# Attention in turns of four key blocks instead of pairs of heads, ahead of a feed-forward network

## The chip, the core and the metric

The kernel runs on one core of one Trainium2 chip. The metric is device time in microseconds of one execution. Engines: PE is TensorE (matmuls; PEld is its weight load), DVE is VectorE, ACT is ScalarE, SP is SyncE, which here only issues transfers (DMAs).

## What is computed

```python
# q, k, v: (8 batches, 12 heads, 448 positions, 64)
scores = scale * np.matmul(q, k.transpose(0, 1, 3, 2)) - np.log(S)
attn = 1.0 / (1.0 + np.exp(-scores))
attn_out = np.matmul(attn, v)
x = attn_out.transpose(0, 2, 1, 3).reshape(B * S, H * D)   # 3584 x 768
h = x @ w_in                                               # 768 x 2048
g = np.maximum(0.01 * h, h)
out = g @ w_out                                            # 2048 x 768
```

The sigmoid takes the place of a softmax, so no sum over keys is needed, and key blocks can be taken in any order.

## The kernel before

Two heads of one batch make a **pair**; there are 48 pairs (`Pair`, from line 348). The 448 keys of a head are three **blocks** of 128 (c = 0, 1, 2) and a rest of 64. For one block PE computes the scores of both heads, side by side in two row halves of the array (64x128 tiles, `sc<-qks`), from q and k split into a high and a low part (high by high, high by low, low by high: three products, so six matmuls a block). ACT takes the sigmoid of both heads at once from PSUM into SBUF (`attn`, line 414, `s<-sc`), and PE multiplies it with v into an accumulator of the pair (`attn_v`, line 427, `pv<-s,v`, 128x64 tiles, two heads side by side). The rests of 64 keys of two neighbouring pairs go together, as four **quarters** of the array (64x64 tiles): `last_scores` (line 419, `sc<-qk`, unsplit) and, in `attn_v`, the products of the rests with v (`pv<-s` on 64x64).

PSUM holds three buffers for scores (`s`, two banks each) and two accumulators (`pv`); the buffers go round in the order in which they are asked for. SBUF holds four raw pairs of q and k (`raws`), two split pairs (`spl`) and six sigmoid blocks (`at`).

The split of a pair is a cast (`high`, line 374, `qks<-qk`, on ACT or, where the plan says so, on DVE) and a subtraction on DVE (`low`, line 378, `qks<-qk,qks`). When a pair's accumulator is complete, ACT copies it to SBUF (`keep`, line 442, `x<-pv`). SP issues all loads (`load_qk`, `load_v`).

The order is written by hand. Every engine works through its own queue in program order. The main loop goes over pairs j, four **slots** each: block 2 of pair j, blocks 0 and 1 of pair j+1, products of pair j with v for blocks 0 and 1, and `ending` (line 646: the product for block 2, and for every second pair the quarters). `later(n, ...)` puts a side task n slots on; `go` (line 637) emits the side tasks that are due, then the slot's matmuls, then as much of `prep()` as `PACES` says: `prep` decodes and sums the weights of the feed-forward network on DVE (`wd`, `ws`) for a product scheme with seven products (`ORDER`). `PLAN_ATTN` puts casts, subtractions and sums of the finished attention outputs (`hi`, `lo`) into slots, `EARLY` calls `advance`, which starts loads and splits of the first weights, in the last pairs.

After the attention comes the feed-forward network: first `x @ w_in` (`px_h`, `py_h`, `pz_h`), then the product with `w_out` (`px_o`, ...); PSUM banks are shared out anew. At the very end the last output block is copied from PSUM by ACT (`c_o<-px_o`) and stored by SP.

Of the kernel before, what the change touches and what calls it, by code (L numbers as in the profile page):

```python
# [27 lines left out]
PACES = 2.2, 2  # L28
# [23 lines left out]
def attn_ffn_kernel(ctx: ExitStack, tc: tile.TileContext, qk, v, w_in, w_out, out):  # L52
# [194 lines left out]
    def give(name):  # L247
# [8 lines left out]
        ("raws", 4), ("spl", 2), ("at", 6)))  # L256
# [91 lines left out]
    class Pair:  # L348


        def __init__(self, i):
            self.i, self.part = i, part(i)
            self.a = []
# [40 lines left out]
        def scores(self, h):  # L394
            todo, acts = [], []
            for c in range(2 * h, min(2 * h + 2, NK - 1)):
                ps = psum("s", f"sc_{self.i}_{c}")

                for cols in HALVES if self.i == h == 0 else (slice(0, S),):
                    for m, (kp, qp) in enumerate(((0, 0), (0, 1), (1, 0))):  # L400
                        for j, me in enumerate(heads):
                            todo.append((c, (m > 0 and c + 1, m, cols.start), dict(
                                out=ps[:, j, cols], lhsT=self.parts[me, kp, 1, c * P:c * P + P],
                                rhs=self.parts[me, qp, 0, cols], start=m == 0 and cols.start == 0,
                                stop=m == 2 and cols.stop == S, skip_group_check=True)))
                acts.append((c, ps))
            if self.i == h == 0:
                todo.sort(key=lambda x: x[1])
            for n, (c, ps) in enumerate(acts):
                for x in todo if self.i == h == 0 and n == 0 else [x for x in todo if x[0] == c and (self.i or h)]:  # L410
                    mm(**x[2])
                self.a.append(self.attn(c, ps))
# [14 lines left out]
        def attn_v(self, h):  # L427
            if h == 0:
                self.pv = psum("pv", f"pv_{self.i}")
            for c in range(2 * h, min(2 * h + 2, NK - 1)):  # L430
                for j, me in enumerate(heads):
                    mm(self.pv[me, :S], lhsT=self.v[:, (NK - 1) * j + c, :], rhs=self.a[c][:, j], start=c == 0, stop=False,
                       skip_group_check=True)
            if h == 1 and self.part == 2:
                x = pairs[self.i - 1]
                for j, me in enumerate(heads):
                    for y, rows in ((x, heads[0]), (self, heads[1])):
                        mm(y.pv[me, :S], lhsT=self.v[rows, 2 * NK - 2 + j, :], rhs=x.last[rows, j],
                           start=False, stop=True, skip_group_check=True)
                later(1, x.keep, self.keep, first=True)  # L440
# [10 lines left out]
    class Operands:  # L451
# [60 lines left out]
        "e13.1": "h002", "e15.1": "l002", "e17.1": "h102", "e19.1": "l102", "e20.1": "s302", "e22.1": "s202", "e24.1": "s402",  # L512
        "e26.1": "s102", "e27.1": "h402", "e29.1": "l402", "e30.1": "h502", "e32.1": "l502", "e33.1": "h302", "e35.1": "l302"}
# [18 lines left out]
    EARLY = {(-4, 0): -8, (-4, 2): -6, (-3, 0): -4, (-2, 0): -3, (-1, 0): -2, (-1, 2): -1, (0, 0): 0}  # L532
# [113 lines left out]
    def ending(j):  # L646

        pairs[j].attn_v(1)
        x = 0 if j == 0 else j + 1
        if x % 2 == 0 and x < last:  # L650
            pairs[x].last_scores()

# [3 lines left out]
    slot(lambda: pairs[0].scores(0))  # L656
    for j in range(last + 1):
# [7 lines left out]
        if j + 4 <= last:  # L665
            later(4, pairs[j + 4].load_qk)
# [112 lines left out]
    for k, (p, n, u0) in enumerate(items):  # L779
# [7 lines left out]
        def work():  # L787
# [7 lines left out]
            for m, (acc, begins) in enumerate(accs):  # L795
# [3 lines left out]
                if ending:  # L799
                    store(p, m, quads[m].done(n))  # L800
# [46 lines left out]
```

## Time and profile before

| | us |
|---|---|
| median of 3 runs (lowest to highest) | 1071.53 (1071.09 to 1071.82) |
| the profiled execution | 1071.87 |
| its span in the trace | 1070.1 |
| busy: PE | 1063.6 (99%) |
| busy: PE weight load | 884.0 (83%) |
| busy: DVE | 672.1 (63%) |
| busy: ACT | 581.4 (54%) |

The profile's page comes from one execution of 1071.87 us. The span runs from the first to the last recorded piece of work. Matmuls follow each other in a pipeline, so that the start of one to the start of the next says more than the duration of one. PE's granted clock is full throughout.

### The profile page before, as it was taken

What the parts mean: (1) busy time and instruction counts of PE and PEld (TensorE: products, weight loads), DVE (VectorE), ACT (ScalarE), POOL (GpSimd) and SP (SyncE); (2) the same over time, 40 slices, a digit from 0 to 9 for tenths busy, and PEclk for the clock granted to TensorE, in tenths of its full rate; (3) what the DMA queues carried; (4) which work ended last, traced back from release to release, by engine and by line L of the source; (5) the groups of instructions that cost most, each with busy time, mean ns of one, the idle gap of its engine ahead of it and who ended that gap; (6) DMA issues with size and microseconds to landing.
All of it is one profiled execution on the core that took longest, in us unless ns stands there. A gap on an engine that the chain in (4) does not pass through costs nothing.

```text
span 1070.1 us, 16067 instructions
## 1 busy us (share of the span) xinstructions
PE 1063.6 (99%) x5882; PEld 884.0 (83%) x5882; DVE 672.1 (63%) x1020; ACT 581.4 (54%) x833; POOL 0.3 (0%) x5
## 2 busy tenths in 40 slices
PE   8999999999999999999999999999999999999998
PEld 5454444545999999999999999999999999999997
DVE  5667878676797898878977666655332423333332
ACT  6787878877554655566555555554333233323332
POOL 0000000000000000000000000000000000000000
PEclk9999999999999999999999999999999999999999
DMA  7787688788899789899898887876544545465552
GB/s 246 251 300 273 240 292 291 254 309 310 247 292 309 210 283 321 273 294 342 256 313 270 265 268 241 318 265 212 184 152 127 184 147 163 121 185 151 152 158 87
DMA packets 107791, 255.61 MB, mean 239 GB/s; under 512 B 11968, under 2 KB 55744, under 8 KB 107712
## 3 DMA queue, kind: packets, MB, share of 16 engines
q1 hardware_dynamic: 107280, 254.13, 72.5%
q8 instruction: 46, 0.75, 0.3%
q10 hardware_dynamic: 432, 0.46, 0.1%
q14 instruction: 33, 0.27, 0.1%
HBM read 167.38 MB, written 87.16 MB: 238 GB/s over the span
## 4 chain that ended last, share of the span: by engine, by line
PE 99%; DMA 1%; DVE 0%; ACTq 0%; ACT 0%; issue 0%; DVEq 0%
PE px_h L85 22%; PE px_o L85 22%; PE pv L85 13%; PE pz_h L85 11%; PE pz_o L85 11%; PE sc L85 11%; PE py_h L85 5%; PE py_o L85 5%; DMA qk<-in_qk 1%; DVE qks L85 0%; ACTq L85 0%; ACT c_o L85 0%; DVEq L85 0%
## 5 line engine op out<-in xcount | busy, mean ns | idle before, releaser
L85 DVE TENSOR_TENSOR gs<-gg,gs 128x896 fp32r<-128x896 f32 x112 | 122.3, 1092 | 226.8 <-ACT gs L85 226.8
L85 PE MATMUL px_o<-gs,w 128*128 128x448 f32 x1152 | 232.5, 362 | 0.0
L85 PE MATMUL px_h<-hi,w 128*128 128x448 f32 x768 | 231.7, 362 | 0.0
L85 PEld LDWEIGHTS px_o<-gs,w 128*128 128x128 f32 x1152 | 216.0, 187 | 14.4
L85 ACT CAST gs<-gg 128x896 fp32r<-128x896 f32 x112 | 105.3, 941 | 220.7 <-PE px_o L85 114.8
L85 ACT ACTIVATE s<-sc 128x896 f32<-128x896 f32 x168 | 150.2, 935 | 47.1 <-PE sc L85 47.1
L85 PEld LDWEIGHTS px_h<-hi,w 128*128 128x128 f32 x768 | 144.0, 187 | 9.7 <-issue 0.7
L85 PE MATMUL pv<-s,v 128*64 128x448 f32 (+1 forms) x768 | 140.7, 551 | 0.0
L85 PE MATMUL px_h<-lo,w 128*128 128x448 f32 x384 | 138.8, 362 | 0.0
L85 DVE TENSOR_TENSOR w<-wx,w 128x768 fp32r<-128x768 f32 (+1 forms) x160 | 136.0, 852 | 3.3 <-ACT w L85 2.8
L85 ACT CAST w<-wx 128x768 fp32r<-128x768 f32 (+1 forms) x160 | 119.6, 751 | 7.1 <-DMA wx<-t 7.0
L85 PE MATMUL pz_h<-hi,w 128*128 128x448 f32 x384 | 118.3, 362 | 0.0
L85 PE MATMUL pz_o<-gs,w 128*128 128x448 f32 x576 | 116.5, 362 | 0.0
L85 PEld LDWEIGHTS pz_o<-gs,w 128*128 128x128 f32 x576 | 108.0, 187 | 7.2
L85 PEld LDWEIGHTS sc<-qks 64*128 64x128 f32 x876 | 76.5, 185 | 42.7 <-issue 31.7
L85 PEld LDWEIGHTS pv<-s,v 128*64 128x64 f32 (+1 forms) x768 | 42.1, 135 | 76.1 <-issue 67.4
L85 PE MATMUL sc<-qks 64*128 64x448 f32 (+1 forms) x876 | 101.8, 373 | 1.8 <-DVE qks L85 1.7
L85 DVE TENSOR_TENSOR qks<-qk,qks 128x832 fp32r<-128x832 f32 (+3 forms) x51 | 49.5, 973 | 56.7 <-ACT qks L85 56.5
L85 ACT COPY c_h<-px_h 128x448 f32<-128x448 f32 x64 | 34.2, 534 | 91.1 <-PE px_h L85 87.6
L85 PEld LDWEIGHTS px_h<-lo,w 128*128 128x128 f32 x384 | 72.0, 187 | 5.4
L85 PEld LDWEIGHTS pz_h<-hi,w 128*128 128x128 f32 x384 | 72.0, 187 | 4.5
L85 DVE SCALAR_TENSOR_TENSOR wd<-wr,wd 128x384 int32<-128x384 int32 x128 | 71.3, 557 | 3.3
(49 smaller groups left out, 951.7 us busy)
## 6 DMA issues: line engine op xcount, KB each, us to landing
gg<-g SPq DMA_DIRECT2D x112, 448.0 KB, 3.5
wx<-t SPq DMA_DIRECT2D x120, 384.0 KB, 4.4
g<-c_h SPq DMA_DIRECT2D x128, 224.0 KB, 4.5
g<-s SPq DMA_DIRECT2D x96, 224.0 KB, 4.5
qk<-in_qk SPq DMA_DIRECT2D x46, 448.0 KB, 5.3
wr<-in_w_in SPq DMA_DIRECT2D x32, 384.0 KB, 3.7
t<-ws SPq DMA_DIRECT2D x16, 768.0 KB, 6.7
wr<-in_w_out SPq DMA_DIRECT2D x32, 384.0 KB, 4.0
```

Of the source, the lines that this page charges most:

```text
L85: return lambda *args, **kw: tc.keep_in_program_order(issue(*args, **kw))
```

## The change

The loop over pairs becomes a loop over 36 **turns** of four key blocks; blocks are numbered through all pairs (block n is block n % 3 of pair n // 3). Turn r has four slots: scores of blocks 4r+1 and 4r+2; scores of 4r+3 and 4r+4; `middle`; products with v of blocks 4r+2 and 4r+3. `middle` emits, in the turns with r % 3 = 0 or 2, the quarters (products of the rests of two pairs with v, then scores of the rests of the next two pairs), and then the products with v of blocks 4r and 4r+1. So the quarters stand between scores and products with v, and no longer between products with v and scores. Turn 0 has an order of its own: the first pair's blocks, the quarters' scores of pairs 0 and 1, the first pair's products with v, then scores of blocks 3 and 4 and `middle`; of the first pair only block 0 is computed in two halves of the columns.

Splits, loads and copies are put into slots by a table (`calls`), copies of accumulators by `DONE`. There are fewer slots, and `prep` gets 2.955 instead of 2.2 steps a slot, which is the same total. `at` has seven buffers. The last output block is copied in two halves, one by ACT, one by DVE, and stored by SP's queue and by ACT's.

```diff
-PACES = 2.2, 2
+PACES = 2.955, 2
...
-        ("raws", 4), ("spl", 2), ("at", 6)))
+        ("raws", 4), ("spl", 2), ("at", 7)))
...
-            self.a = []
+            self.a, self.pv = [], None
...
-        def scores(self, h):
...
+        def scores(self, c):
+            ps = psum("s", f"sc_{self.i}_{c}")
+            cut = HALVES if self.i == c == 0 else (slice(0, S),)
+            for m, (kp, qp) in enumerate(((0, 0), (0, 1), (1, 0))):
+                for cols in cut:
+                    for j, me in enumerate(heads):
+                        mm(ps[:, j, cols], lhsT=self.parts[me, kp, 1, c * P:c * P + P], rhs=self.parts[me, qp, 0, cols],
+                           start=m == 0 and cols.start == 0, stop=m == 2 and cols.stop == S, skip_group_check=True)
+            self.a.append(self.attn(c, ps))
 
...
-        def attn_v(self, h):
...
+        def sums(self):
+            first = self.pv is None
+            if first:
                 self.pv = psum("pv", f"pv_{self.i}")
-            for c in range(2 * h, min(2 * h + 2, NK - 1)):
-                for j, me in enumerate(heads):
-                    mm(self.pv[me, :S], lhsT=self.v[:, (NK - 1) * j + c, :], rhs=self.a[c][:, j], start=c == 0, stop=False,
+            return self.pv, first
+        def attn_v(self, c):
+            pv, first = self.sums()
+            for j, me in enumerate(heads):
+                mm(pv[me, :S], lhsT=self.v[:, (NK - 1) * j + c, :], rhs=self.a[c][:, j], start=first, stop=False,
+                   skip_group_check=True)
+        def last_v(self):
+            y = pairs[self.i + 1]
+            sums = [x.sums() for x in (self, y)]
+            for j, me in enumerate(heads):
+                for (pv, first), rows in zip(sums, heads):
+                    mm(pv[me, :S], lhsT=y.v[rows, 2 * NK - 2 + j, :], rhs=self.last[rows, j], start=first, stop=True,
                        skip_group_check=True)
-            if h == 1 and self.part == 2:
-                x = pairs[self.i - 1]
-                for j, me in enumerate(heads):
-                    for y, rows in ((x, heads[0]), (self, heads[1])):
-                        mm(y.pv[me, :S], lhsT=self.v[rows, 2 * NK - 2 + j, :], rhs=x.last[rows, j],
-                           start=False, stop=True, skip_group_check=True)
-                later(1, x.keep, self.keep, first=True)
 
...
-        "e13.1": "h002", "e15.1": "l002", "e17.1": "h102", "e19.1": "l102", "e20.1": "s302", "e22.1": "s202", "e24.1": "s402",
-        "e26.1": "s102", "e27.1": "h402", "e29.1": "l402", "e30.1": "h502", "e32.1": "l502", "e33.1": "h302", "e35.1": "l302"}
+        "r10.2": "h002", "r11.2": "l002", "r13.2": "h102", "r14.2": "l102", "r15.2": "s302", "r16.2": "s202", "r18.2": "s402",
+        "r19.2": "s102", "r21.2": "h402", "r22.2": "l402", "r23.2": "h502", "r24.2": "l502", "r25.2": "h302", "r26.2": "l302"}
...
-    EARLY = {(-4, 0): -8, (-4, 2): -6, (-3, 0): -4, (-2, 0): -3, (-1, 0): -2, (-1, 2): -1, (0, 0): 0}
+    EARLY = {(-3, 0): -8, (-3, 2): -6, (-2, 0): -4, (-2, 1): -3, (-2, 2): -2, (-1, 0): -1, (-1, 2): 0}
...
-    def ending(j):
-        pairs[j].attn_v(1)
-        x = 0 if j == 0 else j + 1
-        if x % 2 == 0 and x < last:
-            pairs[x].last_scores()
...
-    slot(lambda: pairs[0].scores(0))
-    for j in range(last + 1):
-        works = [lambda: pairs[j].scores(1)] + [lambda: pairs[j + 1].scores(0)] * (j < last)
-        works += [lambda: pairs[j].attn_v(0), lambda: ending(j)]
-        if j + 2 <= last:
-            later(0, pairs[j + 2].load_v)
-            later(1, lambda j=j: pairs[j + 2].high(vcopy if PLAN_ATTN.get(f"e{j}.1", "").startswith("h") else copy))
-            later(2, pairs[j + 2].low)
-        if j + 4 <= last:
-            later(4, pairs[j + 4].load_qk)
+    TURNS = (last + 1) * 3 // 4
+    def run(blocks, kind):
+        for n in blocks:
+            if n < 3 * (last + 1):
+                getattr(pairs[n // 3], kind)(n % 3)
+    def middle(r, blocks):
+        p, n = divmod(r, 3)
+        if n != 1:
+            me = 4 * p + n
+            pairs[me].last_v()
+            if me + 2 < last:
+                pairs[me + 2].last_scores()
+        run(blocks, "attn_v")
+    DONE = {(0, 3): (0,), (1, 2): (1,), (2, 2): (2,), (2, 3): (3,)}
+    calls = {}
+    def call(r, n, fn):
+        calls.setdefault((r, n), []).append(fn)
+    for i in range(2, last + 1):
+        p, n = divmod(i, 4)
+        r, one, two = ((-1, 0, 0), (-1, 2, 3), (0, 2, 3), (1, 2, 3))[n]
+        r += 3 * p
+        call(r, one, lambda i=i, how=vcopy if PLAN_ATTN.get(f"r{r}.2", "").startswith("h") else copy: pairs[i].high(how))
+        call(r, two, pairs[i].low)
+        if i >= 4:
+            r, at_slot = ((0, 2 * (p == 1)), (0, 1 + 2 * (p == 1)), (1, 0), (2, 0))[n]
+            call(3 * p - 3 + r, at_slot, pairs[i].load_qk)
+        r, at_slot = ((1, 0), (1, 3), (2, 3), (3, 0))[n]
+        call(*((3 * p - 3 + r, at_slot) if i >= 4 else (i - 2, 0)), pairs[i].load_v)
+    slot(lambda: run((0,), "scores"))
+    for r in range(TURNS):
+        works = [lambda: run((4 * r + 1, 4 * r + 2), "scores"), lambda: run((4 * r + 3, 4 * r + 4), "scores")]
+        works += [lambda: middle(r, (4 * r, 4 * r + 1)), lambda: run((4 * r + 2, 4 * r + 3), "attn_v")]
+        if r == 0:
+            works = [works[0], pairs[0].last_scores, lambda: run((0, 1), "attn_v"), lambda: run((2,), "attn_v"),
+                     works[1], lambda: middle(0, (3,))]
+            later(len(works), pairs[0].keep, first=True)
         for n, work in enumerate(works):
-            go([(ops[0], PLAN_ATTN.get(f"e{j}.{n}", ""))], work, PACES[0] * (j > 0))
-            t = EARLY.get((j - last, n))
+            later(0, *calls.get((r, n), ()))
+            go([(ops[0], PLAN_ATTN.get(f"r{r}.{n}", ""))], work, PACES[0] * (r > 0))
+            if r and (r % 3, n) in DONE:
+                later(0, *(pairs[4 * (r // 3) + x].keep for x in DONE[r % 3, n]), first=True)
+            t = EARLY.get((r - TURNS, n))
             if t is not None:
                 advance(t)
 
...
-                if ending:
+                if ending and m < NB - 1:
                     store(p, m, quads[m].done(n))
+                elif ending:
+                    t = op.tile([P, S], F32, tag="o", name="end", bufs=8)
+                    b = 2 * p
+                    for cols, how, queue in zip(HALVES, (copy, vcopy), (dma, dma_act)):
+                        how(out=t[:, cols], in_=acc[:, cols])
+                        queue(out=out[NB + m, :, b * S + cols.start:b * S + cols.stop], in_=t[:, cols])
 
```

In the rows below, a name like `sc_17_0` is the score buffer of pair 17, block 0 (block 3: the rests), `s_` its sigmoid, `qks_` a pair's split q and k, `pv_` its accumulator; the last number of a name only tells buffers apart.

PE's queue before, two pairs in the middle of the attention:

```order
L85 MATMUL sc_16_2_1137<-qks_16_1027 128x448 x6
L85 MATMUL sc_17_0_1150<-qks_17_1079 128x448 x6
L85 MATMUL sc_17_1_1151<-qks_17_1079 128x448 x6
L85 MATMUL pv_16_1169<-s_16_0_1091,v_16_1014 64x448 x2
L85 MATMUL pv_16_1169<-s_16_1_1099,v_16_1014 64x448 x2
L85 MATMUL pv_16_1169<-s_16_2_1144,v_16_1014 64x448 x2
L85 MATMUL sc_17_2_1180<-qks_17_1079 128x448 x6
L85 MATMUL sc_18_0_1197<-qks_18_1148 128x448 x6
L85 MATMUL sc_18_1_1198<-qks_18_1148 128x448 x6
L85 MATMUL pv_17_1218<-s_17_0_1158,v_17_1066 64x448 x2
L85 MATMUL pv_17_1218<-s_17_1_1166,v_17_1066 64x448 x2
L85 MATMUL pv_17_1218<-s_17_2_1187,v_17_1066 64x448 x2
```

PE's queue after, from turn 13 to the scores of turn 14:

```order
L85 MATMUL sc_17_2_1197<-qks_17_1081 128x448 x6
L85 MATMUL sc_18_0_1206<-qks_18_1166 128x448 x6
L85 MATMUL sc_18_1_1218<-qks_18_1166 128x448 x6
L85 MATMUL sc_18_2_1227<-qks_18_1166 128x448 x6
L85 MATMUL pv_17_1169<-s_17_1_1162,v_17_1022 64x448 x2
L85 MATMUL pv_17_1169<-s_17_2_1204,v_17_1022 64x448 x2
L85 MATMUL pv_18_1255<-s_18_0_1213,v_18_1106 64x448 x2
L85 MATMUL pv_18_1255<-s_18_1_1225,v_18_1106 64x448 x2
L85 MATMUL sc_19_0_1269<-qks_19_1240 128x448 x6
L85 MATMUL sc_19_1_1278<-qks_19_1240 128x448 x6
L85 MATMUL sc_19_2_1290<-qks_19_1240 128x448 x6
L85 MATMUL sc_20_0_1299<-qks_20_1264 128x448 x6
```

Before, three blocks of scores alternate with three blocks of products; after, four alternate with four, and block 0 of pair 20 is computed ahead of the products of pair 19.

ACT's queue before, around the splits of pairs 44 and 45:

```order
L85 COPY x_13_2518<-pv_41_2604 128x448
L85 ACTIVATE s_42_2_2640<-sc_42_2_2633 128x896
L85 CAST qks_44_2646<-qk_44_2565 128x832
L85 ACTIVATE s_43_0_2656<-sc_43_0_2648 128x896
L85 ACTIVATE s_43_1_2664<-sc_43_1_2649 128x896
L85 ACTIVATE s_43_2_2692<-sc_43_2_2685 128x896
L85 CAST qks_45_2698<-qk_45_2629 128x832
```

ACT's queue after, turn 31 (four sigmoids) and the beginning of turn 32:

```order
L85 ACTIVATE s_41_2_2593<-sc_41_2_2586 128x896
L85 ACTIVATE s_42_0_2602<-sc_42_0_2595 128x896
L85 ACTIVATE s_42_1_2615<-sc_42_1_2608 128x896
L85 ACTIVATE s_42_2_2624<-sc_42_2_2617 128x896
L85 CAST qks_43_2629<-qk_43_2425 128x832
L85 COPY x_13_2506<-pv_41_2555 128x448
L85 CAST qks_44_2652<-qk_44_2510 128x832
L85 ACTIVATE s_43_0_2664<-sc_43_0_2657 128x896
```

Before, each pair's cast stands between the sigmoids of one pair and the next; after, the cast of pair 43 follows four sigmoids in a row, and the cast of pair 44 follows it with one copy between.

DVE's queue before, from the subtraction of pair 43 to that of pair 44 (`wd` is `prep`'s work):

```order
L85 TENSOR_TENSOR qks_43_2580<-qk_43_2520,qks_43_2580 128x832
L85 TENSOR_SCALAR wd1_2_2562<-wr1_2_1_2449 128x384
L85 TENSOR_SCALAR wd1_2_2562<-wd1_2_2562 128x384 x2
L85 SCALAR_TENSOR_TENSOR wd1_2_2562<-wr1_2_1_2449,wd1_2_2562 128x384 x2
L85 TENSOR_SCALAR wd1_2_2562<-wr1_2_2_2495 128x384
L85 TENSOR_SCALAR wd1_2_2562<-wd1_2_2562 128x384 x2
L85 TENSOR_TENSOR qks_44_2646<-qk_44_2565,qks_44_2646 128x832
```

DVE's queue after, the same two subtractions:

```order
L85 TENSOR_SCALAR wd1_2_2571<-wr1_2_2_2490 128x384
L85 TENSOR_TENSOR qks_43_2629<-qk_43_2425,qks_43_2629 128x832
L85 TENSOR_SCALAR wd1_2_2571<-wd1_2_2571 128x384 x2
L85 SCALAR_TENSOR_TENSOR wd1_2_2571<-wr1_2_2_2490,wd1_2_2571 128x384
L85 TENSOR_TENSOR qks_44_2652<-qk_44_2510,qks_44_2652 128x832
L85 SCALAR_TENSOR_TENSOR wd1_2_2571<-wr1_2_2_2490,wd1_2_2571 128x384
```

Before, five groups of `prep`'s instructions stand between the two subtractions; after, two.

## Rows read from the trace of the kernel before

**Rows 1.** Page, chain that ended last: share of the span by engine.

```profile
PE 99%; DMA 1%; DVE 0%; ACTq 0%; ACT 0%; issue 0%; DVEq 0%
```

**Rows 2.** Busy time by stretch: PE, PEld, DVE, ACT, POOL; clock; DMA share; GB/s.

```profile
50.00:100.00 50.00, 50.00 (x368) 25.22 (x362) 34.44 (x68) 40.19 (x53) 0.00 (x0) 1.00 0.77 267
```

**Rows 3.** PE's timeline: start, length, work, count [idle before]; two pairs.

```profile
92.23 0.93 PE L85 MATMUL sc<-qk 64*64 64x448 f32 x8
...
95.11 2.48 PE L85 MATMUL pv<-s,v 128*64 128x448 f32 x12
97.52 2.09 PE L85 MATMUL sc<-qks 64*128 64x448 f32 x18
99.54 3.39 PE L85 MATMUL pv<-s,v 128*64 128x448 f32 x20
102.74 0.93 PE L85 MATMUL sc<-qk 64*64 64x448 f32 x8
```

**Rows 4.** PE's timeline, end of the attention.

```profile
255.62 0.88 PE L85 MATMUL sc<-qks 64*128 64x448 f32 x6
256.42 3.39 PE L85 MATMUL pv<-s,v 128*64 128x448 f32 x20
259.74 0.47 PE L85 MATMUL px_h<-hi,w 128*128 128x448 f32 x1
```

**Rows 5.** Weight loads' timeline, products with v and quarters.

```profile
99.96 0.14 PEld L85 LDWEIGHTS pv<-s,v 128*64 128x64 f32 x2 [0.23 <-issue]
...
101.09 0.14 PEld L85 LDWEIGHTS pv<-s,v 128*64 128x64 f32 x2 [0.23 <-issue]
101.94 0.21 PEld L85 LDWEIGHTS pv<-s,v 64*64 64x64 f32 x8 [0.70 <-issue]
102.37 0.15 PEld L85 LDWEIGHTS sc<-qk 64*64 64x64 f32 x4 [0.22 <-issue]
```

**Rows 6.** PE's timeline, first scores.

```profile
3.98 2.64 PE L85 MATMUL sc<-qks 64*128 64x224 f32 x30
```

**Rows 7.** Chain of waits at the start: start, length, what.

```profile
1.65 5.38 DMA qk<-in_qk
```

**Rows 8.** The load of q and k issued at 6.9: issue and landing.

```profile
L85 SPq DMA_DIRECT2D qk<-in_qk x1: 328/328/328, 6.9 to 6.9; - x1
...
DMA to landing us min/median/max: 6.4/6.4/6.4
```

**Rows 9.** ACT's timeline beside rows 3.

```profile
95.77 0.91 ACT L85 CAST qks<-qk 128x832 fp32r<-128x832 f32 x1
...
98.49 0.93 ACT L85 ACTIVATE s<-sc 128x896 f32<-128x896 f32 x1 [0.18 <-PE sc L85]
...
100.51 1.73 ACT L85 ACTIVATE s<-sc 128x896 f32<-128x896 f32 x2
```

**Rows 10.** Timeline of all engines, a score run that waits for a sigmoid.

```profile
171.14 2.15 PE L85 MATMUL sc<-qks 64*128 64x448 f32 x18
...
172.41 0.50 PEld L85 LDWEIGHTS sc<-qks 64*128 64x128 f32 x6 [0.16 <-ACT s L85]
```

**Rows 11.** DVE's timeline beside rows 3.

```profile
96.71 1.03 DVE L85 TENSOR_TENSOR qks<-qk,qks 128x832 fp32r<-128x832 f32 x1 [1.24 <-ACT qks L85]
...
99.12 0.76 DVE L85 TENSOR_SCALAR wd<-wd 128x384 f32<-128x384 f32 x2
...
100.37 1.15 DVE L85 SCALAR_TENSOR_TENSOR wd<-wr,wd 128x384 int32<-128x384 int32 x2
```

**Rows 12.** SP's loads of q and k, from 15 to 260 us: issue to landing.

```profile
DMA to landing us min/median/max: 3.9/5.3/9.7
```

**Rows 13.** ACT's timeline, the last copy.

```profile
1066.48 0.53 ACT L85 COPY c_o<-px_o 128x448 f32<-128x448 f32 x1 [0.67 <-PE px_o L85]
```

**Rows 14.** The last two stores: issue to landing.

```profile
DMA to landing us min/median/max: 1.9/1.9/1.9
```

**Rows 15.** Page, DMA issues: count, KB each, median us to landing.

```profile
qk<-in_qk ACTq DMA_DIRECT2D x2, 112.0 KB, 2.8
```

More of the change, by code (lines that the diff above doesn't have):

```diff
@@ L392, in split @@
                         sub(low[:, 0, x], self.raw[:, 0, x], high[:, 0, x])
-        def scores(self, h):
-            todo, acts = [], []
-            for c in range(2 * h, min(2 * h + 2, NK - 1)):
-                ps = psum("s", f"sc_{self.i}_{c}")
-                for cols in HALVES if self.i == h == 0 else (slice(0, S),):
-                    for m, (kp, qp) in enumerate(((0, 0), (0, 1), (1, 0))):
-                        for j, me in enumerate(heads):
[L402 to L412, printed above, removed]
+        def scores(self, c):
[7 more added lines that the diff above has]
+            self.a.append(self.attn(c, ps))
         def attn(self, c, ps):
@@ L425, in last_scores @@
             self.last = self.attn(NK - 1, ps)
-        def attn_v(self, h):
-            if h == 0:
+        def sums(self):
+            first = self.pv is None
+            if first:
                 self.pv = psum("pv", f"pv_{self.i}")
-            for c in range(2 * h, min(2 * h + 2, NK - 1)):
-                for j, me in enumerate(heads):
-                    mm(self.pv[me, :S], lhsT=self.v[:, (NK - 1) * j + c, :], rhs=self.a[c][:, j], start=c == 0, stop=False,
-                       skip_group_check=True)
-            if h == 1 and self.part == 2:
-                x = pairs[self.i - 1]
-                for j, me in enumerate(heads):
-                    for y, rows in ((x, heads[0]), (self, heads[1])):
-                        mm(y.pv[me, :S], lhsT=self.v[rows, 2 * NK - 2 + j, :], rhs=x.last[rows, j],
-                           start=False, stop=True, skip_group_check=True)
-                later(1, x.keep, self.keep, first=True)
+            return self.pv, first
[10 more added lines that the diff above has]
+                    mm(pv[me, :S], lhsT=y.v[rows, 2 * NK - 2 + j, :], rhs=self.last[rows, j], start=first, stop=True,
+                       skip_group_check=True)
         def keep(self):
```

## The prediction

> **What bounds the kernel now.** I read the chain that ended last first: it runs through PE for 99% of the span [rows 1], so a change is worth what it takes from PE's queue, less the waits that it puts there. Then a stretch of the attention: PE is busy all the time, DVE 69% and ACT 80% of it [rows 2]; these two have room on average, and the question is whether they are in time at each place. Then PE's timeline over two pairs [rows 3], which gives the price of each step, and the end of the attention [rows 4]: the feed-forward network starts at 259.74. From there only the last block is changed, so the sum is the new time of that start, and the tail.
>
> **Prices.** From start to start, six score matmuls take 256.42 - 255.62 = .80 [rows 4] and eighteen 99.54 - 97.52 = 2.02 [rows 3]. So a block of scores is .61 and a run of them .20 more. A step of products with v (both heads, half of a block) is (101.09 - 99.96) / 3 = .376 [rows 5]; six steps take 97.52 - 95.11 = 2.41 [rows 3], so a run costs .16 beside its steps, and a block .75. The extra is the change of tiles: from the step at 101.09 to the first one on 64x64 tiles are .85 [rows 5], two steps and .10, and that first one takes .43, .05 more than a step. A change to fp32 tiles is thus .15; the run of scores, with the changes at both its ends, shows .20. The quarters are four steps: two of products and two of scores, and between them there is no change (102.37 - 101.94 and 102.74 - 102.37 [rows 3, 5]). With their changes they add (3.20 - 2.41) + .87 = 1.66, with 102.74 - 99.54 = 3.20 and .87 from the rest.
>
> Two pairs are one period of 102.74 - 92.23 = 10.51 [rows 3], so four pairs take 21.02. By the prices: 12 blocks of scores 7.29, 12 of products 9.02, eight quarter steps 3.01, four runs of each kind 1.44, two changes for quarters .33; together 21.1, which agrees.
>
> **Part 1, longer runs.** After the change four pairs are three turns: three runs of each kind instead of four, which is .36 less in 21.02. A turn without quarters is 4 x .61 + .20 + 4 x .75 + .16 = 5.8 (5.78 unrounded), with quarters 7.45 (+1.67). For this the quarters stand between scores and products with v: scores to 64x64 and 64x64 to 128x64 are two neighbourhoods that no row shows. Bounds: nothing for both, or .20 each; I take .15 and .16, which is the nearest change shown, 128x64 to 64x64 [rows 5].
>
> A sentence of the Trainium skill, page "TensorEngine Tiling (Array Packing)", section "Key Properties", says that changing the tiling mode, not just the tile, drains the engine. By it the two unseen changes cost what the shown ones do and the sum stays; without it rival 2 holds. The trace agrees where it shows changes (.15, .20).
>
> **Part 2, the start.** Scores of pair 0 still end near 3.98 + 2.64 = 6.62 [rows 6]. The quarters of pairs 0 and 1 need the load that lands at 1.65 + 5.38 = 7.03 [rows 7]; with a weight load PE starts at 7.2, ends at 8.07. Products of pair 0 (2.41) to 10.48; blocks 0 and 1 of pair 1 (1.41) to 11.89, products of the rests (.80) to 12.69. The next quarters need the q and k issued at 6.9, landing 6.4 later, at 13.3 [rows 8]; from 13.35 their scores take .87 and the block that follows .91: turn 1 starts at 15.13. Turns 1 to 35: 12 x 5.78 + 23 x 7.45, less 1.36 for the last one (three blocks of scores, no scores of rests), is 239.35. **Without new waits the attention ends at 254.5, 5.25 earlier than now.**
>
> **Part 3, the waits that it adds.** Let T be a turn's start.
> (a) *The score banks.* There are three, so the fourth block of a run takes the first one's. A sigmoid starts .97 after its run (98.49 - 97.52), lasts .93 [rows 3, 9], so the bank is free at T + 1.90 and the weight load can go .05 later. Without a wait that load would be at T + 1.72: the load of the third block of a run begins, in [rows 10], at 172.41 - 171.14 = 1.27, of which .16 is such a wait, so 1.11, and a block is .61 more. It is thus .23 late. In [rows 10] a load that was .16 late made the run only .06 longer (2.15 against 2.09 [rows 3]), so PE has .10 of lead: .13 a run. Bounds: 0 (ACT was earlier free than that) and .22. For 34 runs **4.4** (0 to 7.5).
>
> The same page, section "PSUM Bottleneck", warns that tiling makes TensorE faster but not the evacuation of PSUM. Taken by itself it speaks against the change: four blocks at the sigmoids' pace of .80 [rows 9] instead of .61 would be .76 in each of 34 runs, 26 us. The sum does not take that, since three banks let ACT catch up under the products.
>
> (b) *The third pair's cast, in turns without quarters.* Four sigmoids at a pitch of 1.73 - .93 = .80 [rows 9] come before the cast of pair 4p+3 in ACT's queue: it runs from T + 4.2 to 5.1 (.91 [rows 9]), the subtraction (1.03 [rows 11]) to T + 6.17. Turn r+1 starts at T + 5.91; the weight load of its second step, which needs that low part, would go at T + 6.11 (.30 for the first step, .10 of lead) and can go at 6.22 (.05 behind the subtraction): .11 late. Twelve such turns, in three of which DVE makes the cast early: **1.0**. The copies and the cast of pair 4p+4 queue behind it on ACT.
> (c) *The next pair's subtraction.* It stands on DVE behind the former one and `prep`'s work. For pair 44: 6.17, two scalings .76, one combination 1.15 / 2, the subtraction 1.03 [rows 11] give T + 8.55; the fourth block of turn 32 wants it at T + 5.91 + .11 + .20 + 3 x .61 + .20 = 8.25: .3 late. Read in the same way, pair 4 is .5 late, pairs 8 and 12 hardly (.06 each), pair 32, whose cast is DVE's as well, .8, the others not: **1.7**.
> (d) *The last turns.* The first weights' cast and subtraction come before those of pair 47 on ACT and DVE: **.8** (0 to 1.8, a cast and a subtraction by [rows 9, 11]).
> Together 7.9, bounds 0 to 12.
>
> **Part 4, free by their cover.** Of loads of q and k, each is issued at least a turn and a half (about 10 us) before its first reader on PE, against 5.3 in the middle and 9.7 at most to land [rows 12]; SP's order of the others moves by at most a turn. A load that came 1 late would cost about that once. Copies of accumulators have the next run of scores (2.6) as cover for .53 each (a copy of that size [rows 13]). `prep` is the same work over the same slots. The seventh sigmoid buffer covers the block that is computed a turn ahead. At zero together.
>
> **Part 5, the tail.** Half a copy instead of a whole one: between 448 columns (.53 [rows 13]) and 832 (.91 [rows 9]) a column costs .001, so 224 fewer save .2. The store took 1.9 [rows 14]; a half by its share would be about 1 less, while pieces of 112 KB at the start took 2.8 [rows 15], .9 more. I take the .2 alone (-1.2 to +.7).
>
> **Sum.** 259.74 - 5.25 + 7.9 = 262.4 for the start of the feed-forward network, +2.65; with the tail +2.45. Against the profiled execution's 1071.87 (span 1070.1) that is 1074.3; that execution was .34 above the median of 1071.53, so for the median **1074.0**, slower by .23%. A difference within .2% (2.1 us) can hardly be told from none by measuring.
>
> **Rivals.**
> 1. *Casts and subtractions are in time* (b, c, d vanish, the bank stays). For it: they hang on .1 to .8 us each, and ACT idles .18 before a sigmoid and DVE 1.24 before a subtraction [rows 9, 11]. Against: the cast stands after four sigmoids by the order, and nothing moves it. 3.5 less: 1070.5, no change.
> 2. *The unseen tile changes are free.* The rests are already laid out in row halves like the scores. 24 x .15 = 3.6 less: 1070.4, no change. Against: each change shown costs [rows 5].
> 3. *No wait at all, the bank's included.* Three of four sigmoids end under PE's work; if the first ones start earlier than .97 and rival 1 holds too, the whole 7.9 goes: 1066.1, faster by .5%. This is the other side; it decides if the bank is free at T + 1.82, the load's natural 1.72 and its .10 of lead. Against: .97 is PE's pipeline and not a queue.
> 4. *DVE falls behind.* `prep` now comes in denser slots: 69% busy [rows 2] leaves 31%, but two subtractions come close together at each end of three turns. If each of 11 periods loses another .5 (one combination, 1.15 / 2 [rows 11]) to a late subtraction: +5.5, 1079.5.
>
> **How the numbers follow.** Forecast .48 (its bounds are wide: .35 slower, .13 same), rival 1 .19 (.17 same, .02 faster), rival 2 .06 (same), rival 3 .15 (faster), rival 4 .12 (slower). Faster .17, same .36, slower .47. The range leaves out rival 3's end and most of rival 4: 1068.0 to 1077.5.
>
> **What would show it.** In the profile after: runs of 24 score matmuls of 2.75 from start to start (2.62 without (a)), each with a weight load that waits about .2 for ACT's sigmoid; score matmuls that wait for DVE's split at the turns after those without quarters, .1 to .8; turns of 5.9 and 7.6; quarter scores .87 before products; `px_h` first at 262.4. It is wrong if `px_h` starts before 257 or after 267, if the turns without quarters take 5.8, or if the gap between scores and quarters is under .05.

## The result

The changed kernel takes 1073.92 us (median of 10 runs, 1073.50 to 1074.65), the kernel before 1071.47 (10 runs, 1070.93 to 1072.61): a ratio of 1.0021, 95% interval 1.0012 to 1.0029. It is slower by a fifth of a per cent, 2.45 us. The profiled execution of the changed kernel took 1073.58, its span is 1071.8 (before: 1071.87 and 1070.1), so between these two executions the difference is only 1.7: the one before lay .40 above its median, the changed one .34 below.

The chain that ended last, share of the span by engine, on the page of the changed kernel:

```profile
PE 97%; ACT 1%; DVE 1%; issue 0%; DMA 0%; ACTq 0%
```

Before it was PE for 99% [rows 1]. Now ACT and DVE stand in it with 1% each: there PE's queue waits for them. (The chain counts their work at these places, which is more than what PE loses.) A timeline of PE over two turns, one without quarters (from 79.27) and one with (from 85.19): start, length, work, count.

```profile
76.11 3.23 PE L85 MATMUL pv<-s,v 128*64 128x448 f32 x16
79.27 2.83 PE L85 MATMUL sc<-qks 64*128 64x448 f32 x24
82.03 3.23 PE L85 MATMUL pv<-s,v 128*64 128x448 f32 x16
85.19 2.75 PE L85 MATMUL sc<-qks 64*128 64x448 f32 x24
87.87 0.98 PE L85 MATMUL pv<-s,v 64*64 64x448 f32 x8
88.67 0.56 PE L85 MATMUL sc<-qk 64*64 64x448 f32 x4
```

Read from start to start, as in [rows 3], four product blocks take 79.27 - 76.11 = 3.16, as the prices said. The products of the rests take .80 from scores to the next quarters (88.67 - 87.87), two steps of .376 and .05 more, as in the change shown in [rows 5]; the other part of a change, the .10 before the first step, is within the length of the score run. The score runs are 82.03 - 79.27 = 2.76 and 87.87 - 85.19 = 2.68 long; the price without a wait is 2.62. What PE's weight load waited for up to 262 us (us in all, times, longest):

```profile
PEld sc L85 <- ACT s L85: 7.0, 36, 0.3
...
PEld sc L85 <- DVE qks L85: 2.9, 5, 0.9
```

In the kernel before there were six such waits for a sigmoid in the same stretch, one of them in [rows 10]; now there are 36, .2 each, one in nearly every turn. The waits for a subtraction are the other part. Of the full turns, turn 23 has the longest; here all engines (PEld is the weight load):

```profile
169.15 2.50 PE L85 MATMUL sc<-qks 64*128 64x448 f32 x20
...
170.35 0.58 DVE L85 CAST qks<-qk 128x832 fp32r<-128x832 f32 x1
170.97 1.02 DVE L85 TENSOR_TENSOR qks<-qk,qks 128x832 fp32r<-128x832 f32 x1
171.17 0.19 PEld L85 LDWEIGHTS sc<-qks 64*128 64x128 f32 x2 [0.24 <-ACT s L85]
...
172.05 0.30 PEld L85 LDWEIGHTS sc<-qks 64*128 64x128 f32 x4 [0.69 <-DVE qks L85]
172.05 0.68 PE L85 MATMUL sc<-qks 64*128 64x448 f32 x4 [0.40 <-DVE qks L85]
```

The fourth block first waits .24 for the first one's sigmoid, which must have read its bank; then its second step waits .69 for pair 32's subtraction, which DVE begins at 170.97, behind its own cast of that pair. The end of the attention, PE:

```profile
254.23 0.48 PE L85 MATMUL sc<-qks 64*128 64x448 f32 x2
255.32 1.91 PE L85 MATMUL sc<-qks 64*128 64x448 f32 x16 [0.62 <-DVE qks L85]
257.16 4.14 PE L85 MATMUL pv<-s,v 64*64 64x448 f32 x24
261.23 0.47 PE L85 MATMUL px_h<-hi,w 128*128 128x448 f32 x1
```

Pair 47's second step waits for a subtraction that stands behind that of the first weights. The feed-forward network starts at 261.23 instead of 259.74 [rows 4]: +1.49. From its first to its last matmul it takes 806.66 (trace, starts), before 806.34: +.32. From the last matmul to the end of the span 3.91 instead of 3.97. Together +1.75, the difference of the spans.

The score runs of the 34 full turns add up to 6.1 over 2.62 each. Turns are of three kinds by r % 3, of which 0 and 2 have quarters: kind 0, 11 runs of 2.68 to 2.70; kind 1, 12 runs of 2.75 to 2.77; kind 2, 11 runs of 2.68 to 3.51. If .07 (kinds 0 and 2) and .14 (kind 1) are the bank's, it costs 3.2, and the splits 2.9; the last turn adds .9 (its 18 matmuls take 2.93, by the price 2.02). The experiments test this division.

### The profile page after: what moved, and what is told of

The parts are those of the page before. It is cut to its first block, busy times and chain, and to the rows that moved or that the text cites. A ratio compares the mean times of both kernels' runs of the same rounds, so it can differ in the third digit from the quotient of the medians.

```text
span 1071.8 us, 16039 instructions
## 1 busy us (share of the span) xinstructions
PE 1065.7 (99%) x5876; PEld 884.6 (83%) x5876; DVE 672.1 (63%) x1022; ACT 581.4 (54%) x832; POOL 0.3 (0%) x5
## 4 chain that ended last, share of the span: by engine, by line
PE 97%; ACT 1%; DVE 1%; issue 0%; DMA 0%; ACTq 0%
PE px_h L85 22%; PE px_o L85 21%; PE pv L85 12%; PE pz_h L85 11%; PE pz_o L85 11%; PE sc L85 10%; PE py_o L85 5%; PE py_h L85 5%; ACT s L85 1%; DVE qks L85 1%; DMA qk<-in_qk 0%; ACT qks L85 0%; ACT w L85 0%; DVE wd L85 0%; ACT x L85 0%
## 5 line engine op out<-in xcount | busy, mean ns | idle before, releaser
L85 ACT ACTIVATE s<-sc 128x896 f32<-128x896 f32 x168 | 143.4, 926 | 27.3 <-PE sc L85 26.9
```

The lines of the kernel that those rows point to most:

```text
L85: return lambda *args, **kw: tc.keep_in_program_order(issue(*args, **kw))
```

## The experiments

Theory A: longer runs save some 5 us, and each wait that they bring is an extra that can be taken away by itself. Against it: B, ACT and DVE have no room, so a wait that is removed comes back elsewhere; C, a run of 24 is dearer in itself; D, the loss in the feed-forward network has another cause. "Inner part" below is the time from the start of turn 1 to the first `px_h` (246.14 in the changed kernel), which leaves the start out.

### Splits earlier

```diff
...
-        r, one, two = ((-1, 0, 0), (-1, 2, 3), (0, 2, 3), (1, 2, 3))[n]
+        r, one, two = ((-2, 2, 3), (-1, 2, 3), (0, 2, 3), (1, 1, 2))[n]
...
```

> The changed kernel with one edit: the cast of every fourth pair (4p+3) is put between the second and third sigmoid of its turn instead of behind the fourth, the cast of pair 4p+4 behind the fourth sigmoid of that turn instead of at the next turn's start, and their subtractions one slot earlier. Theory A (longer runs save about 5.2 and each wait is an extra that can be taken away by itself): the score runs of turns with r % 3 = 2, 2.68 to 3.51 long in the changed kernel (3.6 above 2.62 in all), become 2.69 each (0.8 in all), the last turns lose their 0.9, the bank waits stay; the feed-forward network starts at about 257.5 instead of 261.2 and the time is 3.7 less than the changed kernel's, about 1070.2. Rival B (ACT and DVE have no room there: the cast that no longer waits delays the third and fourth sigmoid, and what is won at the splits comes back as waits of products or score banks): start at 260 to 261, time within 1 of the changed kernel's 1073.9.

Measured: 1072.60, ratio 1.0003 to the kernel before (.9993 to 1.0012), 1.3 below the changed kernel. Inner part 243.98, 2.2 less. The last turn's loss is gone, runs of turns 2, 5, 8 and 32 are 2.69 to 2.76 instead of 2.87 to 3.29, turn 23 is 3.25 instead of 3.51; but turns 17 and 20, 2.78 before, are 3.13. PE and DVE there (turn 20):

```profile
148.27 2.37 PE L85 MATMUL sc<-qks 64*128 64x448 f32 x20
150.79 0.67 PE L85 MATMUL sc<-qks 64*128 64x448 f32 x4 [0.16 <-DVE qks L85]
```

```profile
146.79 1.55 DVE L85 TENSOR_TENSOR x<-x,x 128x1344 f32<-128x1344 f32 x1
148.26 0.35 DVE L85 TENSOR_SCALAR wd<-wd 128x384 int32<-128x384 int32 x1
148.65 1.15 DVE L85 SCALAR_TENSOR_TENSOR wd<-wr,wd 128x384 int32<-128x384 int32 x2
149.72 1.02 DVE L85 TENSOR_TENSOR qks<-qk,qks 128x832 fp32r<-128x832 f32 x1
```

Ahead of the subtraction that PE waits for stands a sum of finished outputs (1.55), which the table has one slot ahead of the slot to which this subtraction was moved, and `prep`'s work behind it. So of the inner part's expected 3.7 the 1.4 of these turns is missing, and part of B was right: DVE's queue is where it came back. In the profile turn 1 also starts 1.0 later than in that of the changed kernel (16.13 instead of 15.09; the last section takes this up), so that the attention ends at 260.11, within B's range.

### The sums moved as well

```diff
-        "r16.2": "s202", ... "r19.2": "s102", ... "r22.2": "l402", "r23.2": "h502"
+        "r17.2": "s202", ... "r20.2": "s102", ... "r23.2": "l402 h502"
```

> The kernel with earlier splits (e1) with one more edit: three of DVE's operations on finished outputs (128x1344, 1.55 each), which stood ahead of subtractions in turns 16, 19 and 22, go into the turn behind. Theory A (each split wait that was left has such an operation ahead of it on DVE): the score runs of turns 17, 20 and 23, 3.13, 3.13 and 3.25 long, become 2.69; from the start of turn 1 to the end of the attention 242.5 instead of 244.0; time 1071.2, level with the kernel before. Rival B (DVE is simply behind in this stretch, with transfers that land late): the waits go to the turns next to them, and the time stays within .5 of 1072.6.

Measured: 1070.09 (11 runs, 1069.60 to 1071.36), ratio to the kernel before .9981 (.9972 to .9990); inner part 242.66. What the weight loads of scores waited for, from 15 to 262 us:

```profile
PEld sc L85 <- issue: 26.0, 67, 0.7
...
PEld sc L85 <- ACT s L85: 6.5, 34, 0.2
```

No wait for a subtraction is left; turns 17, 20 and 23 are 2.69, 2.68 and 2.75. All runs together are 3.5 over 2.62, and the 34 waits for a bank are still there. So B is out: nearly all of the split waits (2.9 and .9) came from places in two queues, and taking them away gave 3.5 of inner part and 3.8 of the median. The inner part was expected at 242.5; the time comes out 1.1 below the expected 1071.2. This version is faster than both kernels, than the one before by .19%.

### The first sigmoid shorter

```diff
+        def width(self, c):
+            n = 3 * self.i + c
+            return 400 if n > 4 and n % 4 == 1 else S
...
-            act(out=s, in_=ps[:, :, :S], ...)
+            act(out=s[:, :, :w], in_=ps[:, :, :w], ...)
...
-                mm(pv[me, :S], ..., rhs=self.a[c][:, j], ...)
+                mm(pv[me, :w], ..., rhs=self.a[c][:, j, :w], ...)
```

> As e4_sums_moved, and part of the computation is left out: the sigmoid of the first block of each turn from turn 1 on, and the products with v of that block, take 400 of the 448 queries. That makes this sigmoid .095 shorter (96 columns at .001), so the fourth block's bank comes free before PE asks for it, in a turn with a long lead, or .02 late. Theory A (what a run of 24 score matmuls takes over 2.62 is the wait for that bank, 3.2 in all): runs of 2.62 to 2.65 everywhere instead of 2.69 and 2.77, product runs .08 shorter, no score weight load that waits for a sigmoid; from the start of turn 1 to the end of the attention 236.9 (242.5 less 2.9 and less 34 x .08). Rival C (the excess is a price of the long run itself): runs stay at 2.68 or more, 239.8.

Measured: 1066.15 (one run, part of the computation left out), inner part 237.59. Two turns of kinds 1 and 2, PE, and the waits for sigmoids:

```profile
57.36 2.75 PE L85 MATMUL sc<-qks 64*128 64x448 f32 x24
60.04 3.15 PE L85 MATMUL pv<-s,v 128*64 128x448 f32 x16
63.12 2.70 PE L85 MATMUL sc<-qks 64*128 64x448 f32 x24
65.75 0.98 PE L85 MATMUL pv<-s,v 64*64 64x448 f32 x8
```

```profile
PEld sc L85 <- ACT s L85: 0.3, 2, 0.2
```

The waits fall from 34 to 2, and the runs to 60.04 - 57.36 = 2.68 and 65.75 - 63.12 = 2.63. By kind: 2.66 (0), 2.67 (1), 2.63 (2, but for turns 2 and 23 with 2.67 and 2.69). Of the 3.5 over 2.62, 1.2 is left; the shorter products account for 34 x .08 = 2.7, the rest of the 5.1 for the bank's 2.3. So most of the excess is the bank (A), and C holds at most for .01 to .05 a run, whose cause I did not find.

### Sigmoids by head, alone and with earlier splits

```diff
-            act(out=s, in_=ps[:, :, :S], func=AF.Sigmoid, bias=bias, scale=scale)
+            for j in range(2):
+                act(out=s[:, j], in_=ps[j][:, :S], func=AF.Sigmoid, bias=bias, scale=scale)
...
-    psum = banks("ps_a", dict(s=(3, 2), pv=(2, 1)))
+    psum = banks("ps_a", dict(s=(6, 1), pv=(2, 1)))
```

> The changed kernel with one edit: a score block has two PSUM buffers of one bank (one per head, six in all) and two sigmoids, one per head, so that the first bank of a block comes free about .4 earlier. Theory A: the waits of score weight loads for a sigmoid (36, of .2 each, in the changed kernel) vanish and runs without a split wait take 2.62 instead of 2.68 to 2.77, which is about 3 less in all; against that ACT needs .05 to .2 more for a block, so the casts behind four sigmoids come .2 to .8 later and the split waits (2.9 in the changed kernel) grow by 2 to 8. Time 1073 to 1079, with runs of r % 3 = 0 at 2.62 in any case. Rival C (the .07 to .14 that each run is over 2.62 is not the bank but the price of a run of 24 itself): runs of r % 3 = 0 stay at 2.68 or more.

> Both edits of the first two runs together: earlier splits and sigmoids by head. Theory A: no bank wait and no split wait over .3, all score runs near 2.62, the feed-forward network starts at about 254.5 to 256 and the time is 1067 to 1068.5, below the kernel before. Rival B: ACT, with 2 x .45 or more per block instead of .80, becomes what a turn without quarters waits for; start later than 258, time above 1070.5.

Measured: alone 1076.98 (ratio 1.0045, 1.0028 to 1.0062), with earlier splits 1073.91 (1.0021, 1.0011 to 1.0030). The runs got longer, not shorter: 2.74 (kind 0) and 2.81 (kind 1), .05 more than in the changed kernel. My reasoning had a hole: the first head's bank comes free early, but the fourth block also needs the second head's, and that one comes free later. PE and ACT in a turn without quarters:

```profile
80.90 2.88 PE L85 MATMUL sc<-qks 64*128 64x448 f32 x24
```

```profile
81.87 3.60 ACT L85 ACTIVATE s<-sc 128x448 f32<-128x448 f32 x8 [1.07 <-PE sc L85]
```

Eight sigmoids in 3.60 are .55 each at a pitch of (3.60 - .55) / 7 = .44, so the second ends .97 + .44 + .55 = 1.96 after the run's start, where the one for both heads ended at 1.90. So the run follows the end of that sigmoid: some .05 later, .05 longer; in e5, where it is .08 shorter, .03 to .10 shorter. The rest of the loss is ACT's: 3.60 for four blocks instead of 3.35, and the casts behind them later. B holds for this edit, and a sigmoid by heads is no way out.

### The pace of the weight preparation

```diff
-PACES = 2.955, 2
+PACES = 2.939, 2
```

> The changed kernel with two edits in parts of the run that don't touch each other: the last output block is copied whole by ACT and stored by SP as in the kernel before, and the weight preparation gets 2.939 instead of 2.955 steps a slot (411.5 in all during the attention, as before, instead of 413.7). Theory A: the feed-forward network takes 806.34 from its first to its last matmul again, as before (806.66 in the changed kernel, whose DVE reached two preparation steps ahead of a weight's subtraction at 407); from the start of the last copy to the end of the span 3.62, as before, against 3.5 in the changed kernel; the attention's end moves by less than .4. Rival D (the .32 in the feed-forward network comes from the attention's later end, not from the phase of the preparation): 806.66 stays.

> The changed kernel with 2.939 instead of 2.955 steps of weight preparation a slot, and nothing else. In e3 this and the whole last copy gave a stall of 3.6 in turn 17 (DVE waited 3.9 for the store of prepared weights, with pair 24's subtraction behind it) and a feed-forward network without stalls (806.34). Theory A (the phase of the preparation against SP's queue decides both): the stall of some 3 in turn 17 is there again, the feed-forward network takes 806.34, and the time is 1075.5 to 1077, above the changed kernel's. Rival D (the stall was one late transfer of one execution): turn 17 takes under 2.9, time 1073.4 to 1073.7.

Measured: 1078.38 (e3, one run) and 1076.61 (e7, 4 runs, 1074.52 to 1078.43, ratio 1.0038, 1.0023 to 1.0053). The feed-forward network takes 806.36 and 806.33, so its .32 is the preparation's phase. The calculation "2.955 instead of 2.2 a slot is the same total" was off by two steps: 140 slots by 2.955 are 413.7, 187 by 2.2 are 411.4. In both, turn 17 has the stall, 6.32 and 5.31 long, so it is no single late transfer. In e7, DVE and SP's issues:

```profile
119.49 1.02 DVE L85 TENSOR_TENSOR qks<-qk,qks 128x832 fp32r<-128x832 f32 x1 [0.46 <-ACT qks L85]
124.37 0.36 DVE L85 TENSOR_SCALAR wd<-wr 128x384 int32<-128x384 int32 x1 [3.85 <-DMA t<-wd]
```

```profile
115.59 0.33 SPq L85 DMA_DIRECT2D wr<-in_w_in  x1
116.01 0.38 SPq L85 DMA_DIRECT2D v<-in_v  x1
116.45 0.42 SPq L85 DMA_DIRECT2D qk<-in_qk  x1
116.92 0.42 SPq L85 DMA_DIRECT2D t<-wd  x1
```

```profile
127.87 0.47 PE L85 MATMUL sc<-qks 64*128 64x448 f32 x2
130.71 1.48 PE L85 MATMUL sc<-qks 64*128 64x448 f32 x12 [2.37 <-DVE qks L85]
```

The store of prepared weights is now issued behind a load of v and one of q and k (in the changed kernel it went ahead of them, at 114.67), takes 7.4 instead of 5.0 to land, at 124.3, and DVE, which wants to write the same buffer, waits 3.85. Behind it stands the subtraction of pair 23, not of pair 24 as the expectation has it: PE waits for it at the second step of turn 17's run, in pair 23's first block. That is rival 4 of the prediction, by another mechanism than the one I gave: not more work, but a store that is late. A change of .016 in one number brought it about. With e3's whole last copy 3.97 pass from the last matmul to the end of the span, with halves 3.91: the halves are worth .1 at most.

### The preparation's phase without touching the order

```diff
-            go([(ops[0], PLAN_ATTN.get(f"r{r}.{n}", ""))], work, PACES[0] * (r > 0))
+            go([(ops[0], ...)], work, (PACES[0] - 0.55 * (r == TURNS - 1)) * (r > 0))
```

> As e4_sums_moved, with .55 less of a step of weight preparation in each slot of the last turn, so that 411.5 steps fall into the attention as in the kernel before, with the order up to turn 34 untouched. Theory A (the feed-forward network's .26 to .32 beyond 806.34 comes from two preparation steps that DVE reaches ahead of a weight's subtraction): 806.34, and the attention as in e4; time .25 less than e4's, 1069.8 to 1070.0. Rival D (it comes from something else in the changed kernel): 806.6 again.

Measured: 1070.02 (11 runs), ratio .9986 (.9977 to .9995); 806.34 in the feed-forward network, inner part 242.7. D is out. By time the .25 can't be told from e4's.

### The first pairs, and both kernels once more

```diff
-            works = [works[0], pairs[0].last_scores, lambda: run((0, 1), "attn_v"), lambda: run((2,), "attn_v"),
-                     works[1], lambda: middle(0, (3,))]
+            works = [works[0], works[1], pairs[0].last_scores, lambda: run((0, 1), "attn_v"), lambda: run((2,), "attn_v"),
+                     lambda: middle(0, (3,))]
```

> The changed kernel with the order of the first pairs undone in one place: scores of blocks 3 and 4 (pair 1) come right behind those of pair 0, ahead of the quarters and of pair 0's products. Theory A: these scores wait for pair 1's split (until 8.8 on DVE) with nothing else to do on PE; turn 1 starts at 15.9 where TensorE is fast from 5 us on, as in the changed kernel's profile (15.1), and at 16.2 to 16.5 where its first steps are slow until 8 us, as in the profiles of e1 to e3 (15.9 to 16.2); so this part of the change is worth .3 to .8, and all the rest of the run is as in the changed kernel. Rival E: the load that the second quarters wait for (13.3) sets turn 1's start in any order, and turn 1 starts within .2 of the changed kernel's.

> The kernel before, unchanged, in another profiled execution. In seven of eight profiles of kernels with the changed start, TensorE's first score steps go at half pace until about 8 us and turn 1 starts at 15.6 to 16.3, in one (the changed kernel's) until 5 us and it starts at 15.1; the one profile of the kernel before has them fast from 5 us on. Theory A (which pace the start has differs from execution to execution, whatever the kernel): the attention ends within .3 of 259.7 if the first steps are fast from 5 us, and up to 1 later if not. Rival F (the slow pace belongs to the changed start, whose quarters and products come sooner): first steps fast from 5 us again and the end at 259.7.

> The changed kernel, unchanged, in another profiled execution. Theory A: first score steps slow until about 8 us as in seven of eight other profiles, turn 1 starts at 15.9 to 16.3 instead of 15.1, the score runs of each turn within .1 of those of the first profile (turns 2 and 5 3.3, turn 23 3.5, turn 32 3.1), the attention ends at 262.0 to 262.5. Rival F: turn 1 at 15.1 and the end at 261.2 again.

Measured: 1074.48, 1071.11 and 1073.31 (one run each). PE at the start of the changed kernel again, then of e4, then of the undone order:

```profile
4.61 2.24 PE L85 MATMUL sc<-qks 64*128 64x224 f32 x22 [0.16 <-ACT qks L85]
...
15.22 2.09 PE L85 MATMUL sc<-qks 64*128 64x448 f32 x18
```

```profile
4.15 4.12 PE L85 MATMUL sc<-qks 64*128 64x224 f32 x24 [0.24 <-ACT qks L85]
...
15.56 1.71 PE L85 MATMUL sc<-qks 64*128 64x448 f32 x14
```

```profile
4.09 6.00 PE L85 MATMUL sc<-qks 64*128 64x224 f32 x36 [0.18 <-ACT qks L85]
...
15.90 1.28 PE L85 MATMUL sc<-qks 64*128 64x448 f32 x10
```

In both profiles of the changed kernel and both of the kernel before TensorE reaches its full pace near 5 us, in those of all nine variants after 8, so expectation A of the repeats failed; but e3, e4 and e7 issue the same work up to turn 1 as the changed kernel and reach it late, so rival F's reason does not hold either. The undone order starts turn 1 at 15.90, within the 15.54 to 16.27 of the eight variants with the new order, which reach it as late: the .3 to .8 that I expected of the order of the first pairs does not show, and these starts differ by as much among themselves, so its worth stays open. The kernel before ends its attention at 259.03 in the second profile (259.74 in the first; there the load of [rows 7] took 5.38, here 4.79) and the changed kernel at 260.99: +1.96, with +.29 in the feed-forward network and -.05 behind it a difference of 2.2.

## Why the prediction came out right, step by step

The median was forecast at 1074.0 and is 1073.92. The sign and the mechanism were right, as the runs show; that the figures agree to .1 is partly luck, since from profile to profile the difference was 1.7 and 2.2, not 2.45, and terms missed in both directions. The feed-forward network was forecast to start at 262.4 and starts at 261.23 and 260.99. In the first profile (a) is 1.2 below its forecast and the longer runs save .2 more, while splits and last turn cost .3 more.

- *Prices and longer runs.* Right: 3.16 for four product blocks, .80 and .86 for the quarters, 2.62 for a score run (2.63 in e5, kind 2). The saving is there: the inner part of 246.14, less the 6.1 and .9 of the waits, is 239.1, and 239.35 was forecast. Rival 2 is wrong; the unseen changes of tiles cost what the shown ones do, for with the bank's wait taken away in e5 a run before quarters (2.63 and 2.66) is no more than .04 shorter than one before products with v (2.67).
- *The start.* 15.13 forecast, 15.09 and 15.22 measured; in the variants, whose first steps are slow for longer, up to 1.1 more (last section).
- *(a), the banks.* The mechanism was right (36 waits of .2, and runs that follow the sigmoid's end in e2 and e5), the size too large: 4.4 forecast, 3.2 in the trace, of which e5 took away 2.3. Mis-sized was the time from the run's start to the sigmoid, taken as .97 throughout; it is .92 in the other two kinds of turns, where no split wait comes before it (last section). The warning of the Trainium skill that the prediction cites (page "TensorEngine Tiling (Array Packing)", section "PSUM Bottleneck") is borne out here with .07 to .14 a run, not with the .76 that the sigmoids' pace alone would give.
- *(b) and (c), the splits.* 1.0 and 1.7 forecast, .9 and 1.9 measured in the first profile, .5 and 1.9 in the second, if a run's lateness up to its fourth block is (b) and what comes after is (c). The subtraction of (b) was forecast to end at T + 6.17, .26 after the next run's start; it ends .22 to .25 after it, and the run is .06 to .09 late, not .11, in every full turn where it was forecast, but for turn 5 of the first profile. In (c) pairs 4, 32 and 44 were forecast .5, .8 and .3 late and are .5, .75 and .3; pairs 8 and 12, forecast .06 each, are .1. In turn 5 of the first profile (b) is .5, which was not forecast: pair 7's subtraction begins late, behind `prep`'s work, for which DVE had waited 3.63 until a store of prepared weights had landed. In the second profile DVE goes on sooner and the run is 2.88 long instead of 3.28; so the .9 agrees with the 1.0 by luck. DVE's wait, its subtraction, and PE:

```profile
38.83 0.36 DVE L85 TENSOR_SCALAR wd<-wr 128x384 int32<-128x384 int32 x1 [3.63 <-DMA t<-wd]
...
42.14 1.02 DVE L85 TENSOR_TENSOR qks<-qk,qks 128x832 fp32r<-128x832 f32 x1
```

```profile
42.54 0.47 PE L85 MATMUL sc<-qks 64*128 64x448 f32 x2
43.22 2.67 PE L85 MATMUL sc<-qks 64*128 64x448 f32 x22 [0.20 <-DVE qks L85]
```

  e1 and e4 show that nearly all of (b) and (c) goes with other places in the queues, which the prediction had as "by the order, and nothing moves it".
- *(d), the last turn.* .8 forecast, .9 measured, gone in e1.
- *Part 4.* Loads were covered as said. Wrong was "`prep` is the same work over the same slots", put at zero: the total is two steps higher, which costs .3 near 408 and 534 us, in the feed-forward network, where I had expected nothing.
- *The tail.* .2 forecast, .06 measured: the halves are copied one behind the other, ACT .35, then DVE .39, since DVE waits for ACT.

```profile
1068.29 0.35 ACT L85 COPY end<-px_o 128x224 f32<-128x224 f32 x1 [0.67 <-PE px_o L85]
...
1068.66 0.39 DVE L85 COPY end<-px_o 128x224 f32<-128x224 f32 x1 [9.11 <-ACT end L85]
1069.09 0.35 ACTq L85 DMA_DIRECT2D out<-end  x1
```

- *Rivals 1, 3 and 4.* 1 and 3 are refuted by the waits in the trace. What rival 1 would have given came when the queues were put in order (1070.1 against 1070.5); rival 3's 1066.1 came in no run of the whole computation. It needed the bank free at T + 1.82; the first sigmoid ends at 1.84 in the better turns (.92 after the run's start, .92 long) and at 1.90 or later in the others. Rival 4 did not happen as forecast, but a late store, which brought it about in e7, already cost .4 in turn 5 of the first profile.

## What to carry to other kernels

Before runs of equal work are made longer to save changeovers, count what each run takes from a ring of buffers: here the saving came as the prices said, and the first buffer, which came free too late, was paid for in every run. Then go through each side queue as it will stand and ask which short item, on whose result the main engine waits, now has more ahead of it; here that was worth 3.8 us, more than the change itself. A number that only sets a pace also sets what meets what in the queues, in later parts of the program too, so compare its total exactly.

## What the runs showed of the hardware that was not expected

The sigmoid of a run's first block does not always begin at the same time after the run, though PE's steps up to there are the same. In the changed kernel, with a cast until 86.01 (run from 85.19), and after an idle time of 1.07 (run from 100.22):

```profile
85.08 0.93 ACT L85 CAST qks<-qk 128x832 fp32r<-128x832 f32 x1
86.10 3.35 ACT L85 ACTIVATE s<-sc 128x896 f32<-128x896 f32 x4
```

```profile
101.19 3.35 ACT L85 ACTIVATE s<-sc 128x896 f32<-128x896 f32 x4 [1.07 <-PE sc L85]
```

That is .91 and .97 after the run's start, and the score runs are 2.68 and 2.75 long. In the first profile it is .92 in all turns of kind 0, behind an idle time of .3, and .97 or .98 in all of kind 1, mostly behind 1.08. That idleness makes the difference is not shown: in turn 1 it is .97 after only .38.

TensorE's first score steps have two paces. 24 of them take 2.7 from 3.97 on in the changed kernel and 4.04 (4.15 to 8.19) in e4, while the granted clock is given as 1.00 in both. A step on half the columns takes .21 at first and .11 later, so the first pace is half of the other; it ends near 5 us in the profiles of the two kernels and between 8 and 10 in those of the nine variants. In all of them small matmuls on zeros come before, to about 3.9; the first score begins at 3.97 to 4.07 in the former and at 4.02 to 4.20 in the latter. What decides is open. It moved the start of turn 1 by .3 to 1.2 between programs that do the same there.
